# Three score buffers, a shorter inverse factor and a new order in an attention stage of one core

## Chip, core and metric

One of the eight cores of one Trainium2 chip runs the whole program. The metric is the device time of one execution in microseconds. PE is the matmul engine (TensorE), DVE VectorE, ACT ScalarE, POOL GpSimd, and SP the queue that issues the DMAs.

## What is computed

Attention with a cut on its scores, and two feed-forward layers after it. B = 4 batches, 8 heads, 576 tokens, head size 64, so x has 2304 rows and 512 columns.

```
scores = q @ k.T / 8
scores = where(scores >= max(scores) - tau, scores, -1e9)
attn   = exp(scores - max);  attn = attn / (sum(attn) + 1e-9)
x      = attn @ v                      # heads side by side: 2304 x 512
x      = (silu(x @ w_gate) * (x @ w_val)) @ w_out      # 512 -> 1536 -> 512
out    = relu(x @ w_in)**2 @ w_out2                    # 512 -> 2048 -> 512
```

All products are built from a high and a low part of each operand (kh and kl of a key, and so on), since the matmul's operand types hold too few bits for one part.

## The kernel before

The kernel first does the attention, beside it part of the first feed-forward layer, and then the rest of both layers. It is written with a planner: the program below is traced in program order, and the planner puts each engine's instructions into a fixed queue at build time. It goes by priority (the place in the program, moved forward or back by the numbers in the tables `early0` for batch 0 and `early` for the later ones: a positive number brings a step forward, a negative one puts it back by so many places) and by when each step is ready in its own model. On the chip each queue runs in that order and waits for semaphores. `issue_after` puts an instruction behind another one of the same queue, without a wait for its end.

The attention works on 144 tiles of 128 query rows: per batch four pairs of heads, and nine tiles a pair (four of each head, and one, "T", that holds the last 64 rows of both). Turn i of the loop at line 919 takes these steps on the tiles around i, in this order:

- RED (L685, VectorE): the maximum of a tile's scores, less tau.
- CUT (L693, ScalarE): cuts the scores against it, into z. It is the last reader of the score buffer.
- EXP (L701, ScalarE): exponential into e, and the row sum.
- RCP of tile i-1 (L706, VectorE): r = 1/sum, and from batch 1 on a second VectorE instruction, rs = r * 32768 (L709).
- NORM of tile i-1 (L717, GpSimd): e * rs in fp16, the high part of `both`.
- LO of tile i-2 (L764, VectorE): what the fp16 number lacks, the low part of `both`. It reads e and the high part.
- XT of tile i-2 (L768): a DMA transpose of `both` into `pt`, issued by SP.
- QK of tile i+1 (L675, PE): four matmuls (eight for a T tile) into a score buffer.
- `work(i)`: the attention product of a part (AV, L787, 14 matmuls, six turns after its tile), and one group of the first feed-forward layer (L257, 12 matmuls, or L299, 15) when its inputs are there and the credit of 2600 columns a turn allows. These groups are called fill work below.
- The steps that prepare the next pair of heads (`pair_steps`): load raw q and k, scale and split the query (L592, L598), split the key (kh on ScalarE, kl on GpSimd at L77), copy the rest rows (`tail`), and for the values (`value_steps`, `values`) copies on ScalarE, differences on GpSimd and two DMAs into `vb` (L519, L520).

PSUM has eight banks. A score buffer takes two, so the two of them (`sps`) take four. The other four (`bank`) hold, in batch 0, transposed tiles in the first two and AV in the others; from tile 40 on all four go round among AV and the feed-forward groups (class `Mm`). A group's bank is read by ScalarE, VectorE or both after its last matmul: tanh (L277) and an add (L278) for a gate group, a product (L287) for a value group, a copy (L796) and an add (L802) for an AV, a copy (L69) for an output group. These are emitted one turn or more after the group.

Of the kernel before, what the change touches and what calls it, by code (L numbers as in the profile page):

```python
# [10 lines left out]
F32 = mybir.dt.float32  # L11
# [6 lines left out]
AF = mybir.ActivationFunctionType  # L18
# [4 lines left out]
P = 128  # L23
# [60 lines left out]
def attention_moe(tc, qk, values_, tau, w1, w2, out, cfg):  # L84
# [349 lines left out]
    psum = p1.enter_context(tc.tile_pool(name="psum", bufs=1, space=PSUM))  # L434
    bank = [psum.tile([P, 512], F32, name=f"bank{j}") for j in range(4)]
    mp1 = Mm(bank[3:])
# [30 lines left out]
    def raw_head(h):  # L467
        return rawp.tile([P, 2 * S], F32, name=f"raw{h}", tag=f"raw{h % 2}")
# [53 lines left out]
    def first_pair():  # L522

        for h in range(2):
# [56 lines left out]
            yield s2  # L581

    def pair_steps(p):

        raws = [raw_head(2 * p + j) for j in range(2)]

        def query(j):
            hd, q = head(2 * p + j), raws[j][:, :S]
            if p < NPAIR:
                nc.gpsimd.tensor_scalar(hd["qs"], q, scalar1=qscale, scalar2=1.0, op0=ALU.mult, op1=ALU.mult)  # L590
            else:
                nc.scalar.activation(hd["qs"], q, AF.Copy, scale=qscale)  # L592

        def key(j):
            hd, q = heads[2 * p + j], raws[j][:, :S]
            ops.copy(cfg["kh"], hd["kh"], raws[j][:, S:])
            low = hd["qs"][D:, :]
            nc.vector.scalar_tensor_tensor(  # L598
                low, q[D:, :], qscale[D:, :], low.bitcast(F32), op0=ALU.mult, op1=ALU.subtract
            )  # L600

        def key_low(j, c):
            hd = heads[2 * p + j]
            ops.sub(cfg["kl"], hd["kl"][:, c], raws[j][:, S:][:, c], hd["kh"][:, c].bitcast(F32))

        halves_ = (slice(0, HS), slice(HS, S))
        nc.sync.dma_start(raws[0], qk[2 * p])
        yield None
        nc.sync.dma_start(raws[1], qk[2 * p + 1])
        yield None  # L610
        query(0)
        yield None
        key(0)
        yield None
        key_low(0, halves_[0])
        yield None
        key_low(0, halves_[1])
        tail(heads[2 * p])
        yield None
        if p < NPAIR:  # L620
            values(heads[2 * p], 2 * p)
        query(1)
        yield "next"
        key(1)
        key_low(1, halves_[0])
        yield None
        key_low(1, halves_[1])
        tail(heads[2 * p + 1])
        if p < NPAIR:
            values(heads[2 * p + 1], 2 * p + 1)  # L630
        yield None
# [3 lines left out]
    def value_steps(i):  # L635
        p, k = divmod(i, 9)
        if k == 6 and NPAIR <= p + 1 < B * NPAIR:
            rawv[p + 1] = rawp.tile([P, 2 * VW], F32, name=f"rawv{p + 1}", tag="rawv")
            nc.sync.dma_start(rawv[p + 1], values_[p + 1])
        if k in (3, 5) and NPAIR <= p < B * NPAIR:  # L640
            h = 2 * p + (k == 5)
            values(heads[h], h, rawv[p])

# [16 lines left out]
    st = [dict() for _ in range(NTILE + 8)]  # L660

    def QK(t):
        b, p, i = tiles[t]
        kind, c = ORDER[i]
        ha, hb = (heads.get(b * H + 2 * p + j) for j in range(2))
        sp = sps[t % 2]
        st[t]["s"] = sp
# [29 lines left out]
    def EXP(t):  # L697
        e = es[t % len(es)]
        st[t]["e"] = e
        sum_ = sm.tile([P, 1], F32, name=f"sum{t}", tag="sum")  # L700
        ex = nc.scalar.activation(e, st[t]["z"], AF.Exp, scale=-SLOPE, accum_out=sum_)  # L701
        st[t].update(sum=sum_, exp=ex.ins)

    def RCP(t):
        r = st[t]["r"] = sm.tile([P, 1], F32, name=f"r{t}", tag="r")
        nc.vector.reciprocal(r, st[t]["sum"])  # L706
        if way(t) == "VV":
            rs = st[t]["rs"] = sm.tile([P, 1], F32, name=f"rs{t}", tag="rs")
            nc.vector.tensor_scalar(rs, r, scalar1=UNIT, scalar2=None, op0=ALU.mult)  # L709

    def NORM(t):
        e = st[t]["e"][:, :S]
        r = st[t]["r"]
        if way(t) == "VV":
            a = st[t]["both"] = both[(t + 1) % len(both)]
            rs = st[t]["rs"]
            norm = nc.gpsimd.tensor_scalar(a[:, :S], e, scalar1=rs, scalar2=1.0, op0=ALU.mult, op1=ALU.mult)  # L717
            st[t]["norm"] = norm.ins
            return
# [41 lines left out]
    def LO(t):  # L761

        e, a, r = (st[t][x] for x in ("e", "both", "rs"))
        nc.vector.scalar_tensor_tensor(a[:, S:], e[:, :S], r, a[:, :S], op0=ALU.mult, op1=ALU.subtract)  # L764
# [154 lines left out]
    for i in range(NTILE + late):  # L919
# [3 lines left out]
        if i == cfg["three"] + lag:  # L923
            mp1.banks = deque(bank[2:])
        if i == 9 * NPAIR + lag + 2:
            mp1.banks.extend(bank[:2])
        if i >= cfg["ldat"] and (i % cfg["lev"] == 0 or i >= 9 * NPAIR):
# [23 lines left out]
        at_(mp1.flush, "A", name="FA")  # L951
        if i + 1 < NTILE:
            at_(QK, i + 1)
        work(i)
# [676 lines left out]
def pack(inputs):  # L1631
# [14 lines left out]
    def cols(w, nf):  # L1646
# [48 lines left out]
    "early": {  # L1695
        "TR": 8, "LD": -21, "FD": 4, "NEG": -4, "FA": -19, "PL": -12, "PS": -25, "PH": 6, "LS": 64, "RCP": -8,
        "FP": -40, "NORM": -25, "LP": -100,
    },
# [27 lines left out]
```

## Time and profile before

| | us |
|---|---|
| median of 3 runs | 1162.25 |
| lowest and highest | 1160.58, 1162.57 |
| profiled execution | 1160.94 |
| its span, first to last instruction | 1159.1 |

The page of the profile gives busy times for the whole span. The table by stage gives them for stretches of it, here the three batches with fill work (from the cut of tile 36 to that of tile 143), what is left of the attention, and the rest. The views of waits name, for an engine, which line stood idle and which instruction ended that; the view by line gives counts and mean durations; the timeline gives single instructions in order of time.

### The profile page before, as it was taken

To read this page: it belongs to the slowest core of one execution; us is meant where nothing else is said; L and a number is where in the kernel's file an instruction comes from. 1 tells how busy PE (TensorE), PEld (TensorE's weight loads), DVE (VectorE), ACT (ScalarE), POOL (GpSimd) and SP (SyncE) were. 2 spreads that over 40 slices of the span, in tenths; PEclk is the share of its full clock that TensorE was granted. 3 is DMA by queue.
4 is the path that set the end of the run, shared out by engine and by line. 5 is a ranking of instruction groups with operands and counts; after the bars stand their busy time and mean duration, and the time that the engine had idled before them with its cause. 6 is when DMAs were issued, how large, how long until landed. Compare 5 with 4: busy or idle time off the path is not lost.

```text
span 1159.1 us, 18607 instructions
## 1 busy us (share of the span) xinstructions
PE 1085.5 (94%) x6224; PEld 958.6 (83%) x6224; DVE 886.2 (76%) x2103; ACT 640.3 (55%) x1449; POOL 300.1 (26%) x402
## 2 busy tenths in 40 slices
PE   5999888888888889999999999999999999999998
PEld 4787767777777779998888888888999999989997
DVE  5999898888778785589986887679647768866554
ACT  5999776777667663455433443245546555544221
POOL 5866785766656553000000000000000000000000
PEclk9999999899999989999999999999999999999999
DMA  6444887788767653232220134356364544444552
GB/s 192 134 138 138 166 164 166 153 175 171 138 149 145 134 113 56 65 100 83 82 88 13 37 119 161 102 163 247 144 210 164 181 144 169 162 156 143 183 172 82
DMA packets 177024, 159.43 MB, mean 138 GB/s; under 512 B 133792, under 2 KB 138144, under 8 KB 176928
## 3 DMA queue, kind: packets, MB, share of 16 engines
q1 hardware_dynamic: 176784, 158.24, 49.5%
q8 instruction: 49, 0.80, 0.3%
q14 instruction: 47, 0.39, 0.1%
q10 hardware_dynamic: 144, 0.00, 0.0%
HBM read 100.93 MB, written 22.28 MB: 106 GB/s over the span
## 4 chain that ended last, share of the span: by engine, by line
PE 61%; DVE 3%; POOL 1%; issue 1%; ACT 1%; POOLq 0%; ACTq 0%
PE mm L257 18%; PE mm L1536 17%; PE mm L1483 14%; PE mm L299 9%; PE bank L257 1%; PE bank L299 1%; PE bank L787 1%; DVE st__113 L685 0%; POOL both L717 0%; DVE right L77 0%; DVE sum L1369 0%; ACT z L693 0%; DVE both L764 0%; DVE h L1470 0%; DVE wa L77 0%
## 5 line engine op out<-in xcount | busy, mean ns | idle before, releaser
L693 ACT ACTIVATE z<-s,thr 128x576 f32<-128x576 f32 x144 | 106.1, 737 | 77.0 <-DVE st__113 L685 42.5
L764 DVE SCALAR_TENSOR_TENSOR both<-e,rs,both 128x576 f16<-128x576 f32 x108 | 108.1, 1003 | 42.5 <-POOL both L717 41.7
L675 PE MATMUL s<-kh,qs 128*128 128x288 f32 x256 | 86.8, 352 | 44.9 <-ACT z L693 38.2
L257 PE MATMUL mm<-xs,wa 128*128 128x512 f32 (+2 forms) x672 | 125.8, 347 | 0.5 <-ACT x L69 0.5
L685 DVE TENSOR_SCALAR_CACHE_REDUCE st__113<-s,tau_c 128x576 bf16<-128x576 f32 x144 | 116.3, 808 | 10.3 <-ACT vs L69 5.8
L257 PEld LDWEIGHTS mm<-xs,wa 128*128 128x128 f32 x672 | 109.5, 188 | 15.7 <-ACT x L69 0.7
L717 POOL TENSOR_SCALAR both<-e,rs 128x576 f16<-128x576 f32 x108 | 87.5, 812 | 69.0 <-DVE rs L709 26.9
L257 PE MATMUL bank<-xs_m,wa 128*128 128x288 f32 x576 | 93.0, 309 | 8.8 <-DVE xs_m L77 3.7
L701 ACT ACTIVATE e<-z 128x577 f32<-128x577 f32 x144 | 98.4, 683 | 4.1 <-DVE both L764 0.3
L675 PEld LDWEIGHTS s<-kh,qs 128*128 128x128 f32 x256 | 50.6, 198 | 57.2 <-ACT z L693 48.3
L257 PEld LDWEIGHTS bank<-xs_m,wa 128*128 128x128 f32 x576 | 84.2, 198 | 11.9 <-DVE xs_m L77 7.6
L675 PE MATMUL s<-kl,qs 128*128 128x288 f32 x256 | 76.0, 311 | 0.0
L1553 DVE TENSOR_TENSOR xF<-xF,mm 128x512 f32<-128x512 f32 x54 | 36.9, 684 | 51.0 <-PE mm L1536 51.0
L257 PE MATMUL mm<-xs,wb 128*128 128x512 f32 (+1 forms) x360 | 74.9, 368 | 0.0
L257 PEld LDWEIGHTS mm<-xs,wb 128*128 128x128 f32 x360 | 62.8, 188 | 11.3
L69 ACT ACTIVATE wb<-wf 128x256 fp32r<-128x256 f32 x82 | 34.0, 415 | 65.3 <-DVE wf L1138 38.7
L1536 PE MATMUL mm<-wb,wx 128*128 128x512 f32 x270 | 67.3, 389 | 0.0
L1483 PE MATMUL mm<-right,wb 128*128 128x384 f32 x348 | 65.3, 335 | 1.2 <-DVE right L77 1.2
L1135 ACT ACTIVATE wf<-wr 128x256 f32<-128x256 f32 x64 | 27.6, 433 | 66.3 <-DMA wr<-in_w_dram 51.3
L1470 DVE TENSOR_TENSOR h<-mm,h 128x384 f32<-128x384 f32 x72 | 39.6, 551 | 30.4 <-PE mm L1483 30.4
L1483 PEld LDWEIGHTS mm<-right,wb 128*128 128x128 f32 x348 | 60.8, 188 | 1.9 <-DVE right L77 1.4
L77 POOL TENSOR_TENSOR kl<-raw,kh 128x288 fp32r<-128x288 f32 x62 | 60.4, 991 | 5.9 <-ACT kh L69 5.9
(159 smaller groups left out, 2630.3 us busy)
## 6 DMA issues: line engine op xcount, KB each, us to landing
wr<-in_w_dram SPq DMA_DIRECT2D x106, 256.0 KB, 3.0
raw<-in_qk_dram SPq DMA_DIRECT2D x30, 576.0 KB, 4.2
xF<-in_w_dram SPq DMA_DIRECT2D x30, 256.0 KB, 3.2
right<-kept1T SPq DMA_DIRECT2D x8, 768.0 KB, 5.3
right<-kept0T SPq DMA_DIRECT2D x7, 768.0 KB, 5.6
right<-kept SPq DMA_DIRECT2D x6, 768.0 KB, 4.7
right<-kept2T SPq DMA_DIRECT2D x6, 768.0 KB, 5.6
wa<-kept2T SPq DMA_DIRECT2D x6, 768.0 KB, 5.3
```

Source lines behind the costliest of these rows:

```text
L77: e.tensor_tensor(out, a, b, op=ALU.subtract)
L257: mm(pt[:, :n], w[:, a, col + c * P : col + (c + 1) * P], xs[:, b, c, :], start=(i == 0), stop=(i == len(TERMS) - 1),)
L299: mm(pt[:, :n], ws[k][:, a, 2 * DM + m * P : 2 * DM + (m + 1) * P], us[k][:, b, :], start=(k == 0 and i == 0), stop=(k == ahead and i == 2),)
L675: mm(sp[:, cols], l, r[:, cols], start=(n_ == 0), stop=(n_ == len(pairs) - 1),)
L685: red = nc.vector.tensor_scalar(st_, st[t]["s"][:, :S], scalar1=tau_c, scalar2=None, op0=ALU.subtract, op1=ALU.max, accum_out=th)
L693: nc.scalar.activation(z[:, :S], st[t]["s"][:, :S], AF.Prelu, bias=st[t]["thr"], scale=-1.0, alpha=1 / SLOPE)
L701: ex = nc.scalar.activation(e, st[t]["z"], AF.Exp, scale=-SLOPE, accum_out=sum_)
L717: norm = nc.gpsimd.tensor_scalar(a[:, :S], e, scalar1=rs, scalar2=1.0, op0=ALU.mult, op1=ALU.mult)
L764: nc.vector.scalar_tensor_tensor(a[:, S:], e[:, :S], r, a[:, :S], op0=ALU.mult, op1=ALU.subtract)
L1470: return ("D", read(lambda: nc.vector.tensor_tensor(h, bank[:, :BK], h, op=ALU.add), bank))
L1483: mm(bank[:, :BK], w[:, a, c * P : (c + 1) * P], t[:, b, c, :], start=(n == 0 and x in ("11", "12", "S1")), stop=(n == 5), skip_group_chec ...
L1536: mm(pt, u[:, b, s * P : (s + 1) * P], w[a], start=(half == 0 and j == 0 and i == 0), stop=(half == 1 and j == 1 and i == 2),)
```

## The change

From batch 1 on (tile `THIRD` = 38) the scores go round in three buffers, the third made of the first two of the four other banks, and QK runs two tiles ahead of the loop; AV and the feed-forward groups keep the other two banks, as they had at the end of batch 0. ScalarE divides the row sum by 32768 right behind the exponential, so the reciprocal is the scaled factor and L709 goes; NORM and LO read it. The loads of q and k are issued right behind the last reader of their buffer, a load of values behind that of the next queries, and the value copies behind the exponential of the tile before. The second head's key step comes one step earlier. In the table of priorities RCP and NORM lose their entries (-8, -25) and LO gets -10.

```diff
-    bank = [psum.tile([P, 512], F32, name=f"bank{j}") for j in range(4)]
+    two = psum.tile([P, 1024], F32, name="bank01")
+    bank = [two[:, :512], two[:, 512:], *(psum.tile([P, 512], F32, name=f"bank{j}") for j in range(2, 4))]
...
+    raws, loads = {}, {}
     def pair_steps(p):
-        raws = [raw_head(2 * p + j) for j in range(2)]
+        def load(h):
+            if h not in raws and h < B * H:
+                raws[h] = raw_head(h)
+                loads[h] = nc.sync.dma_start(raws[h], qk[h]).ins
...
-        nc.sync.dma_start(raws[0], qk[2 * p])
-        yield None
-        nc.sync.dma_start(raws[1], qk[2 * p + 1])
+        load(2 * p)
+        load(2 * p + 1)
...
         tail(heads[2 * p])
+        load(2 * p + 2)
         yield None
         if p < NPAIR:
             values(heads[2 * p], 2 * p)
         query(1)
+        yield None
+        key(1)
         yield "next"
-        key(1)
         key_low(1, halves_[0])
+        key_low(1, halves_[1])
         yield None
-        key_low(1, halves_[1])
         tail(heads[2 * p + 1])
+        load(2 * p + 3)
...
-            nc.sync.dma_start(rawv[p + 1], values_[p + 1])
+            with tc.issue_after(loads[2 * p + 2]):
+                nc.sync.dma_start(rawv[p + 1], values_[p + 1])
...
-            values(heads[h], h, rawv[p])
+            with tc.issue_after(st[i - 1]["exp"]):
+                values(heads[h], h, rawv[p])
...
+    THIRD = 9 * NPAIR + 2
+    sps3 = [*sps, two[:, 512 - HS :]]
     def QK(t):
-        sp = sps[t % 2]
+        sp = sps[t % 2] if t < THIRD else sps3[(t - THIRD) % 3]
...
         ex = nc.scalar.activation(e, st[t]["z"], AF.Exp, scale=-SLOPE, accum_out=sum_)
+        if way(t) == "VV":
+            part = sm.tile([P, 1], F32, name=f"part{t}", tag="part")
+            nc.scalar.activation(part, sum_, AF.Copy, scale=1 / UNIT)
+            sum_ = part
...
         nc.vector.reciprocal(r, st[t]["sum"])
-        if way(t) == "VV":
-            rs = st[t]["rs"] = sm.tile([P, 1], F32, name=f"rs{t}", tag="rs")
-            nc.vector.tensor_scalar(rs, r, scalar1=UNIT, scalar2=None, op0=ALU.mult)
...
-        if i == 9 * NPAIR + lag + 2:
-            mp1.banks.extend(bank[:2])
...
-        if i + 1 < NTILE:
-            at_(QK, i + 1)
+        for j in (i + 1, i + 2) if i == THIRD + 1 else (i + 2,) if i > THIRD else (i + 1,):
+            if j < NTILE:
+                at_(QK, j)
...
-        "TR": 8, "LD": -21, "FD": 4, "NEG": -4, "FA": -19, "PL": -12, "PS": -25, "PH": 6, "LS": 64, "RCP": -8,
-        "FP": -40, "NORM": -25, "LP": -100,
+        "TR": 8, "LD": -21, "FD": 4, "NEG": -4, "FA": -19, "PL": -12, "PS": -25, "PH": 6, "LS": 64,
+        "FP": -40, "LO": -10, "LP": -100,
```

## Rows read from the trace of the kernel before

**Rows 1.** The page, busy us, share of the span and instructions of each engine.

```profile
PE 1085.5 (94%) x6224; PEld 958.6 (83%) x6224; DVE 886.2 (76%) x2103; ACT 640.3 (55%) x1449; POOL 300.1 (26%) x402
```

**Rows 2.** Table by stage: stretch, length, busy us by engine, granted clock, DMA.

```profile
101.20:215.30 114.10, 97.26 (x677) 85.57 (x676) 98.09 (x243) 83.17 (x190) 80.72 (x100) 0.99 0.80 164
215.30:326.10 110.80, 94.19 (x660) 82.48 (x660) 95.09 (x231) 81.29 (x182) 73.08 (x90) 0.95 0.78 157
326.10:438.10 112.00, 95.22 (x661) 83.69 (x662) 91.22 (x228) 77.19 (x176) 65.89 (x87) 0.95 0.66 134
438.10:472.40 34.30, 34.30 (x263) 32.92 (x261) 12.38 (x28) 9.84 (x27) 8.17 (x12) 1.00 0.23 38
472.40:1159.00 686.60, 680.88 (x3495) 604.02 (x3493) 505.87 (x1164) 305.60 (x681) 0.00 (x0) 1.00 0.39 134
```

**Rows 3.** Waits of PE, 101.2 to 438.1: total us, times, longest us.

```profile
PE s L675 <- ACT z L693: 36.8, 30, 3.7
```

**Rows 4.** Waits of ScalarE, the same stretch.

```profile
ACT z L693 <- DVE st__113 L685: 42.5, 33, 4.2
ACT z L693 <- DVE r L706: 17.2, 7, 3.7
ACT z L693 <- DVE rs L709: 13.3, 11, 3.0
```

**Rows 5.** Waits of VectorE, the same stretch.

```profile
DVE both L764 <- POOL both L717: 39.4, 52, 2.2
...
DVE st__113 L685 <- PE s L675: 1.0, 2, 0.8
```

**Rows 6.** Waits of GpSimd, the same stretch.

```profile
POOL both L717 <- DVE rs L709: 24.6, 21, 2.3
POOL both L717 <- ACT e L701: 13.1, 8, 2.4
```

**Rows 7.** VectorE by line, the same stretch: count, busy us, mean ns, idle before.

```profile
L764 DVE SCALAR_TENSOR_TENSOR both<-e,rs,both 128x576 f16<-128x576 f32 x105 | 105.2, 1004 | 40.1 <-POOL both L717 39.4
...
L709 DVE TENSOR_SCALAR rs<-r 128x1 f32<-128x1 f32 x106 | 15.7, 149 | 1.4
```

**Rows 8.** The tile `both`, the same stretch: ns least/median/most.

```profile
L764 DVE SCALAR_TENSOR_TENSOR both<-e,rs,both x105: 803/819/1489, 105.6 to 435.9; 128x576 f16<-128x576 f32 x105
```

**Rows 9.** Timeline, all engines: start, us, engine, line, what; idle before and releaser.

```profile
394.31 0.40 PE L675 MATMUL s<-kh,qs 128*128 128x288 f32 x1 [0.43 <-ACT z L693]
...
394.94 1.76 PE L257 MATMUL bank<-xs_m,wa 128*128 128x288 f32 x12
...
395.87 2.16 POOL L77 TENSOR_TENSOR kl<-raw,kh 128x288 fp32r<-128x288 f32 x2 [0.34 <-ACT kh L69]
...
398.02 0.74 POOL L717 TENSOR_SCALAR both<-e,rs 128x576 f16<-128x576 f32 x1
...
398.79 0.82 DVE L764 SCALAR_TENSOR_TENSOR both<-e,rs,both 128x576 f16<-128x576 f32 x1 [1.06 <-POOL both L717]
...
399.89 0.82 DVE L685 TENSOR_SCALAR_CACHE_REDUCE st__113<-s,tau_c 128x576 bf16<-128x576 f32 x1
...
400.81 0.74 ACT L693 ACTIVATE z<-s,thr 128x576 f32<-128x576 f32 x1 [2.75 <-DVE st__113 L685]
401.19 0.46 DVE L287 SCALAR_TENSOR_TENSOR m_th<-m_th,bank 128x288 f32<-128x288 f32 x1
...
401.60 0.40 PE L675 MATMUL s<-kh,qs 128*128 128x288 f32 x1 [2.47 <-ACT z L693]
...
402.92 1.35 DVE L764 SCALAR_TENSOR_TENSOR both<-e,rs,both 128x576 f16<-128x576 f32 x1 [0.31 <-POOL both L717]
...
403.62 1.31 POOL L77 TENSOR_TENSOR rawv<-rawv,vs 128x320 f32<-128x320 f32 x1
```

**Rows 10.** ScalarE by line and shape, 101.2 to 438.1: its smallest instructions.

```profile
L701 ACT ACTIVATION_READ_ACCUMULATOR e<-z 128x1 f32 x107 | 20.4, 191 | 0.0
...
L796 ACT ACTIVATE xF<-bank 64x64 f32<-64x64 f32 x11 | 2.4, 219 | 0.3
```

**Rows 11.** Waits in the SP queue, 160 to 450: total us, times, longest us.

```profile
SPq L607 <- POOL kl L77: 11.7, 6, 3.0
```

More of the change, by code (lines that the diff above doesn't have):

```diff
@@ L581, in first_pair @@
             yield s2
+    raws, loads = {}, {}
     def pair_steps(p):
-        raws = [raw_head(2 * p + j) for j in range(2)]
+        def load(h):
+            if h not in raws and h < B * H:
+                raws[h] = raw_head(h)
+                loads[h] = nc.sync.dma_start(raws[h], qk[h]).ins
         def query(j):
-            hd, q = head(2 * p + j), raws[j][:, :S]
+            hd, q = head(2 * p + j), raws[2 * p + j][:, :S]
             if p < NPAIR:
@@ L594, in key @@
         def key(j):
-            hd, q = heads[2 * p + j], raws[j][:, :S]
-            ops.copy(cfg["kh"], hd["kh"], raws[j][:, S:])
+            hd, q = heads[2 * p + j], raws[2 * p + j][:, :S]
+            ops.copy(cfg["kh"], hd["kh"], raws[2 * p + j][:, S:])
             low = hd["qs"][D:, :]
@@ L603, in key_low @@
             hd = heads[2 * p + j]
-            ops.sub(cfg["kl"], hd["kl"][:, c], raws[j][:, S:][:, c], hd["kh"][:, c].bitcast(F32))
+            ops.sub(cfg["kl"], hd["kl"][:, c], raws[2 * p + j][:, S:][:, c], hd["kh"][:, c].bitcast(F32))
         halves_ = (slice(0, HS), slice(HS, S))
-        nc.sync.dma_start(raws[0], qk[2 * p])
-        yield None
-        nc.sync.dma_start(raws[1], qk[2 * p + 1])
+        load(2 * p)
+        load(2 * p + 1)
         yield None
@@ L715, in NORM @@
             a = st[t]["both"] = both[(t + 1) % len(both)]
-            rs = st[t]["rs"]
-            norm = nc.gpsimd.tensor_scalar(a[:, :S], e, scalar1=rs, scalar2=1.0, op0=ALU.mult, op1=ALU.mult)
+            norm = nc.gpsimd.tensor_scalar(a[:, :S], e, scalar1=r, scalar2=1.0, op0=ALU.mult, op1=ALU.mult)
             st[t]["norm"] = norm.ins
@@ L761, in LO @@
     def LO(t):
-        e, a, r = (st[t][x] for x in ("e", "both", "rs"))
+        e, a, r = (st[t][x] for x in ("e", "both", "r"))
         nc.vector.scalar_tensor_tensor(a[:, S:], e[:, :S], r, a[:, :S], op0=ALU.mult, op1=ALU.subtract)
```

## The prediction, made before the change was run

> **What bounds the kernel now.** I read the page first: PE is busy for 94% of the span [rows 1], so what can be won is PE's idle time, and the question is where it lies. The table by stage answers that [rows 2]: from 438.1 us to the end PE idles 5.7 us in 721, while in the three attention stretches of batches 1 to 3 (101.2 to 438.1 us, 336.9 us, 108 tiles, 3.12 us a tile) it is busy 97.26 + 94.19 + 95.22 = 286.7 us and idle 50.2. The change acts almost only there. In the same stretch DVE is busy 284.4 us, ACT 241.7, POOL 219.7: PE and DVE stand level at 85%.
>
> The waits, engine by engine, tell who sets the pace. PE's one large wait is the score matmul (QK, L675) for the cut on ScalarE (CUT, L693) to give its score buffer free: 36.8 us [rows 3]. ScalarE waits at the cut for VectorE: 42.5 + 17.2 + 13.3 us [rows 4]. VectorE waits for GpSimd's normalised tile (NORM, L717) before it can form the low part (LO, L764): 39.4 us in 52 of 105 tiles, and for the scores of PE hardly at all, 1.0 us [rows 5]. GpSimd in turn waits for VectorE's scaled factor (L709) 24.6 us and for the exponential 13.1 us [rows 6]. So VectorE's queue sets the pace: its own 284.4 us plus 39.4 us behind GpSimd are 96% of the stretch. The timeline shows one case [rows 9]: the scores of tile 131 are begun at 394.31, but VectorE stands 1.06 us at LO until NORM ends at 398.76 (GpSimd had the key's low part before it), only then runs the maximum of tile 131 (399.89), ScalarE had waited 2.75 us for that, and PE 2.47 us for ScalarE.
>
> **The change, part by part.** All terms are for that stretch; the sign is that of the time.
>
> *A. The scaled factor leaves VectorE.* 106 instructions at 149 ns, 15.7 us [rows 7], go from the queue that sets the pace. I take -15.7; bounds 0 (were PE to become the limit at once) and -15.7.
>
> *B. Order: RCP and NORM are no longer put back by 8 and 25 places, LO is put back by 10.* NORM comes earlier on GpSimd, before key and value work that was ahead of it (the 2.16 us of kl ahead of it in [rows 9]), and VectorE reaches LO later. What can go is the 39.4 us of [rows 5]. A queue's order is fixed at build time, and 13.1 us of NORM's own waits are for the exponential [rows 6], which doesn't move. I take half, -20; bounds 0 and -39.4.
>
> *C. LO beside GpSimd.* LO takes 0.82 us in [rows 9] at 398.79 and 1.35 us at 402.92, where GpSimd works on m_u and rawv; the median is 0.819 and the mean 1.004 us [rows 7, 8], so slow ones already cost 105 x 0.185 = 19.4 us. A LO that waits has GpSimd just finishing beside it; one that comes later finds it in its next instruction. Bounds: all at 0.82, -19.4; all at 1.35, 105 x 0.346 = +36. I take half as much again as today, +9, nearer to the mean of today than to either end. The Trainium skill (SBUF — State Buffer, "Who interferes with whom") says that a VectorE instruction with two SBUF inputs contends with a GpSimd instruction that reads SBUF; LO is of that form, and the two durations agree with it. By that rule term C would be at its upper end for every LO that overlaps, which is rival 2.
>
> *D. ScalarE forms sum/32768.* 108 more instructions of one column. The nearest rows are the accumulator read, 191 ns, and the 64x64 copy, 219 ns [rows 10]: 20 to 24 us more on ScalarE. Behind it in the queue stand the next cut and the copies; ScalarE's 73 us of waiting for VectorE [rows 4] cover it, and if that cover is gone it costs up to +24. On the path to NORM one ScalarE instruction replaces one of VectorE: 0.2 against 0.15 us. I take +2.
>
> *E. Three score buffers, two banks for the rest.* QK of tile i+2 is issued in turn i, in three buffers. It waits for the cut of tile i-1, just as QK of tile i+1 in two buffers did: PE's 36.8 us [rows 3] don't go by the count, only by a faster VectorE. What the third buffer gives is a tile's more slack between QK and the maximum, and that wait is 1.0 us [rows 5]. The price: the attention products, the gate/value groups and the output groups turn in two banks, where before it was four. I paired each such group of PE (113 from 101.2 us on) with its last reader in the timeline: mean 2.26 us from first to last matmul, and 4.37 us more until the bank is read; in [rows 9] the group at 394.94 ends at 396.70 and is read until 401.65. With two banks 69 of the 113 groups would have begun before their bank was free, by 134 us in all. Most of that delay is queue order which PE's lead permits, and PE has 36.8 us of waits to spend on it. Bounds: 0, all absorbed; +40, rival 1. A gain by E alone I bound with -1.0. I take +10, a quarter.
>
> *F. Loads and values.* The loads of q and k are issued as soon as the buffer is read, behind GpSimd's kl. The SP queue holds them in order, so a waiting load holds up the DMA transposes and vb copies behind it: such waits are 11.7 us now [rows 11], and PE would only feel them through the products six turns later. The value copies are put behind the previous tile's exponential on ScalarE, which keeps the cut from standing behind them; they wait for GpSimd anyway. Key work of the second head comes one step earlier, same instructions. I take 0; bounds -8 and +5 (a transposed tile that lands late).
>
> *G. The tail.* From 438.1 to 472.4 PE is busy without a gap [rows 2]; with two banks a group's readers have the other group's time, 1.76 us [rows 9], for a tanh and an add of about 0.45 each. I take +1; bounds 0 and +8 (some 20 groups by 0.4).
>
> Sum: -15.7 - 20 + 9 + 2 + 10 + 0 + 1 = -13.7 us. The profiled execution took 1160.9 us (its span 1159.1, 1.8 around it): 1147.2. The median of the runs is 1.3 us above the profiled one, so I say **1148.5 us**, -1.2%. PE would then be idle about 36 of 323 us in the stretch, which it can be.
>
> **Rivals.**
> 1. *The bank rotation takes the place of the freed waits; slower.* A bank is held 2.26 + 4.37 = 6.6 us; two banks give a group each 3.3 us, 113 x 3.3 = 375 against 336.9 us: +38 to +40. With A to D at -25 this ends near +13 to +15, 1175 us. For it: today's mean. Against it: the readers are late because nothing pressed them, and ScalarE and VectorE reach them in the next two turns. It decides if a group's readers stay later than about 3.7 us behind its end: 2 x 2.98 us (336.9/113) less 2.26.
> 2. *GpSimd beside VectorE takes back what the order gives.* LO always at 1.35: -15.7 - 39.4 + 36 + 13 (D, E, G) = -6: 1156 us.
> 3. *VectorE is freed fully and PE becomes the bound.* A and B at their ends with C, D and G as in the sum: -15.7 - 39.4 + 9 + 2 + 1 = -43; PE's idle time is 50.2 us and a twentieth of the stretch stays idle, so about -33: 1129 us.
> 4. *The order isn't moved in the queues* (NORM still behind kl and m_u, which are ready sooner). Then A alone stands against D, E and G: -15.7 + 13 = -3, 1159.5, not to be told from no change.
>
> **How the numbers follow.** Forecast (1138 to 1154) 0.40, rival 3 0.12, rival 2 0.12, rival 4 0.11, rival 1 0.25. About 0.2%, 2.3 us, is what a measurement of this kernel can tell from no change, so of rival 4 a third falls to faster: faster 0.68, same 0.08, slower 0.24 (rival 1, less the part of it in which the banks only eat the gain). The range reaches half into rival 3 and to the price of rival 1: 1130 to 1176, which leaves out some 0.06 and 0.1. It takes in the bounds of each term alone; all of them at one end together it doesn't.
>
> **What would show it.** Right: from about 105 us to the last cut some 323 instead of 337 us; no scaled-factor instruction on VectorE and one more of about 0.2 us on ScalarE per tile (A, D); VectorE's wait at LO at or under 20 us (B); LO's mean at 1.05 to 1.15 us (C); PE's waits at QK under 30 us, and waits of the groups L257, L299 and L787 for ScalarE's and VectorE's reads of a bank of 5 to 20 us, where now there are hardly any (E); none of these after the last cut (G). Wrong: PE waiting over 40 us for banks, or ScalarE and VectorE standing at tanh and adds for PE (rival 1); LO's mean near 1.35 (rival 2); a wait at LO still near 39 us (rival 4); PE idle under 25 us in the stretch (rival 3). The forecast also falls if the transposed tiles come late, seen as PE waiting for DMA.

## The result: 0.9% slower, and where the 10 us lie

The changed kernel took 1171.9 us in the median (1170.7 to 1174.2), the one before 1162.4 beside it on the same chip: ratio 1.0086, 95% interval 1.0067 to 1.0106. The profiled execution has a span of 1168.9 us against 1159.1.

The table by stage puts the loss in place. It is cut as in [rows 2], at the cut of tile 36 and at that of tile 143, and at the first matmul of the second stage (columns: stretch, length, busy us of PE, PEld, DVE, ACT, POOL, granted clock, DMA share, GB/s). After:

```profile
99.10:442.50 343.40, 283.83 (x1987) 249.77 (x1986) 277.37 (x589) 253.67 (x655) 221.67 (x279) 0.97 0.75 150
442.50:483.20 40.70, 39.23 (x281) 36.17 (x280) 11.60 (x27) 11.07 (x29) 8.36 (x12) 0.96 0.13 25
```

Before, cut in the same way:

```profile
101.20:438.10 336.90, 286.67 (x1998) 251.75 (x1998) 284.40 (x700) 241.65 (x548) 219.70 (x277) 0.96 0.75 152
438.10:473.20 35.10, 34.65 (x264) 33.04 (x261) 12.38 (x28) 10.63 (x28) 8.17 (x12) 1.00 0.23 38
```

Batch 0 ends 2.1 us sooner, batches 1 to 3 take 6.5 us more, the tail up to the second stage 5.6 us more, and the rest is the same within 0.2 us: +9.8. Of the 6.5 us some 2 are work moved over a border from batch 0 (the run on the loads, below). VectorE has 111 instructions less in the attention stretch and 7.0 us less to do, and still the stretch is longer. PE stands idle 59.6 us in it, where it was 50.2.

The waits say what became of PE's 36.8 us at the scores [rows 3]. Waits of PE after, 99.1 to 442.5 (total us, times, longest us):

```profile
PE bank L800 <- DVE xF L815: 19.3, 13, 4.0
PE bank L257 <- DVE xF L815: 10.2, 9, 2.4
PE bank L257 <- DVE m_th L278: 9.4, 11, 1.8
PE bank L299 <- DVE xF L815: 9.0, 3, 4.1
...
PE bank L800 <- DVE m_th L278: 2.7, 3, 1.1
...
PE s L688 <- ACT z L706: 0.5, 2, 0.3
```

The wait for the cut is gone (0.5 us, and 1.0 us for the third buffer). In its place PE waits some 51 us for VectorE to read the two banks in which attention products (L800) and feed-forward groups (L257, L299) go round. The waits of the other three engines, the same stretch, each line from its own view:

```profile
DVE both L777 <- POOL both L730: 51.5, 61, 2.4
```
```profile
ACT z L706 <- DVE st__112 L698: 60.2, 42, 3.8
```
```profile
POOL both L730 <- DVE r L723: 60.3, 44, 4.4
```

VectorE waits longer at the low part (LO) than before, 51.5 against 39.4 us [rows 5], though the new order was to shorten that. GpSimd waits 60.3 us for the factor, where it was 24.6 [rows 6]. ScalarE's waits at the cut are the exception: with another 2.2 us for the reciprocal they come to 62.4 us, where they were 73.0 [rows 4].

One place of the timeline after shows all of it at once (start, us, engine, what; idle before and releaser):

```profile
321.77 0.74 POOL L730 TENSOR_SCALAR both<-e,r 128x576 f16<-128x576 f32 x1 [3.03 <-DMA pt<-both]
...
322.55 1.33 DVE L777 SCALAR_TENSOR_TENSOR both<-e,r,both 128x576 f16<-128x576 f32 x1 [2.38 <-POOL both L730]
...
323.91 0.42 DVE L815 SCALAR_TENSOR_TENSOR xF<-bank,xF 64x256 f32<-64x256 f32 x1
324.36 0.16 DVE L723 RECIPROCAL r<-part 128x1 f32<-128x1 f32 x1
324.39 1.85 PE L299 MATMUL bank<-m_u,wa 128*128 128x288 f32 x12 [2.46 <-DVE xF L815]
324.44 0.80 DVE L698 TENSOR_SCALAR_CACHE_REDUCE st__112<-s,tau_c 128x576 bf16<-128x576 f32 x1
...
325.29 0.74 ACT L706 ACTIVATE z<-s,thr 128x576 f32<-128x576 f32 x1 [0.95 <-DVE st__112 L698]
```

The high part (NORM) of tile 105 waits on GpSimd 3.03 us for a buffer that a DMA transpose still reads. The low part of that tile stands at the head of VectorE's queue and waits 2.38 us for NORM. Behind it in the queue stand the add that frees a bank (L815), for which PE waits 2.46 us, and the maximum of tile 107, for which ScalarE waits; the scores of tile 107 were begun at 321.24. A wait at LO is paid by whatever is queued behind it. That NORM waits for a transpose is the rarer reason in this kernel, three places in all, against 44 waits for the reciprocal:

```profile
POOL both L730 <- DMA pt<-both: 5.9, 3, 3.0
```

### The profile page after: what moved, and what is told of

Read it like the earlier page. It is cut to its first block, busy times and chain, and to the rows that moved or that the text cites. A ratio compares the mean times of both kernels' runs of the same rounds, so it can differ in the third digit from the quotient of the medians.

```text
span 1168.9 us, 18539 instructions
## 1 busy us (share of the span) xinstructions
PE 1088.5 (93%) x6224; PEld 959.6 (82%) x6224; DVE 879.7 (75%) x1995; ACT 653.0 (56%) x1557; POOL 302.7 (26%) x402
## 4 chain that ended last, share of the span: by engine, by line
PE 56%; DVE 11%; POOL 9%; issue 6%; ACT 5%; DMA 3%; POOLq 0%; ACTq 0%; DVEq 0%; SPq 0%
PE mm L257 17%; PE mm L1548 15%; PE mm L1495 11%; PE mm L299 7%; POOL both L730 4%; DVE both L777 2%; PE bank L257 2%; POOL kl L77 2%; DMA pt<-both 2%; PE bank L299 2%; DVE st__112 L698 2%; PE bank L800 2%; DMA wr<-in_w_dram 1%; ACT z L706 1%; ACT e L714 1%
## 5 line engine op out<-in xcount | busy, mean ns | idle before, releaser
L777 DVE SCALAR_TENSOR_TENSOR both<-e,r,both 128x576 f16<-128x576 f32 x108 | 110.1, 1022 | 53.9 <-POOL both L730 53.4
L257 PE MATMUL mm<-xs,wa 128*128 128x512 f32 (+2 forms) x672 | 125.7, 347 | 0.5 <-ACT x L69 0.5
L257 PEld LDWEIGHTS mm<-xs,wa 128*128 128x128 f32 x672 | 109.4, 188 | 15.7 <-ACT x L69 0.7
L257 PE MATMUL bank<-xs_m,wa 128*128 128x288 f32 x576 | 94.2, 310 | 24.0 <-DVE m_th L278 9.7
L730 POOL TENSOR_SCALAR both<-e,r 128x576 f16<-128x576 f32 x108 | 92.7, 859 | 70.2 <-DVE r L723 62.8
L257 PEld LDWEIGHTS bank<-xs_m,wa 128*128 128x128 f32 x576 | 82.2, 195 | 33.7 <-DVE m_th L278 11.7
L706 ACT ACTIVATE z<-s,thr 128x576 f32<-128x576 f32 x109 | 80.2, 736 | 46.0 <-DVE st__112 L698 43.8
L698 DVE TENSOR_SCALAR_CACHE_REDUCE st__112<-s,tau_c 128x576 bf16<-128x576 f32 x109 | 88.1, 808 | 5.2 <-PE s L688 3.3
L688 PE MATMUL s<-kh,qs 128*128 128x288 f32 x210 | 68.0, 337 | 9.4 <-DVE qs L545 6.3
L257 PE MATMUL mm<-xs,wb 128*128 128x512 f32 (+1 forms) x360 | 74.9, 368 | 0.0
L257 PEld LDWEIGHTS mm<-xs,wb 128*128 128x128 f32 x360 | 62.9, 188 | 11.3
L688 PE MATMUL s<-kl,qs 128*128 128x288 f32 x210 | 61.8, 309 | 0.0
L1479 ACT ACTIVATE h<-mm 128x384 f32<-128x384 f32 x72 | 34.9, 484 | 47.8 <-PE mm L1495 47.4
L800 PE MATMUL bank<-pt,vs 128*128 128x256 f16 (+1 forms) x240 | 39.9, 297 | 22.9 <-DVE xF L815 19.3
```

Of the source, the lines that this page charges most:

```text
L257: mm(pt[:, :n], w[:, a, col + c * P : col + (c + 1) * P], xs[:, b, c, :], start=(i == 0), stop=(i == len(TERMS) - 1),)
L688: mm(sp[:, cols], l, r[:, cols], start=(n_ == 0), stop=(n_ == len(pairs) - 1),)
L698: red = nc.vector.tensor_scalar(st_, st[t]["s"][:, :S], scalar1=tau_c, scalar2=None, op0=ALU.subtract, op1=ALU.max, accum_out=th)
L706: nc.scalar.activation(z[:, :S], st[t]["s"][:, :S], AF.Prelu, bias=st[t]["thr"], scale=-1.0, alpha=1 / SLOPE)
L730: norm = nc.gpsimd.tensor_scalar(a[:, :S], e, scalar1=r, scalar2=1.0, op0=ALU.mult, op1=ALU.mult)
L800: mm(o[:, :n], v, pt[:, k if k < 9 else k - 9, lo : lo + n], start=(k == 0), stop=(k == 13))
```

## Experiments

Each kernel is held against runs of the kernel before on the same chip, whose median lay between 1160.6 and 1162.0 us there. Two variants that were not run side by side are compared through that, so a difference between them is good to 2 or 3 us, by their intervals. The theories: 1, the rotation of groups in two banks costs the time; 2, the new priorities do; 3, ScalarE's added instruction does; 4, any new queue order does; 5, formed after the first runs, the place of LO in VectorE's queue does.

### Two banks alone

```diff
-        if i == 9 * NPAIR + lag + 2:
-            mp1.banks.extend(bank[:2])
```

> The kernel before with one line less: attention products and feed-forward groups keep two banks in batches 1 to 3; two score buffers, the two freed banks stay unused. Theory 1 (the bank rotation makes the change slower): 8 to 20 us slower than before, about 1170 to 1182, PE waiting 30 to 60 us for reads of a bank at L257, L299, L787 and under 15 us at the scores, where it was 36.8. Theory 2 (the order of reciprocal, high part and low part makes it slower): within 4 us of before, since PE's waits only change their name.

1169.5 us, ratio 1.0076 (1.0061 to 1.0091): +8.8 us. Waits of PE, 100.7 to 447.7:

```profile
PE bank L787 <- DVE xF L802: 14.7, 10, 3.0
PE s L675 <- ACT z L693: 9.1, 11, 2.8
PE bank L299 <- DVE xF L802: 8.0, 4, 2.6
PE bank L257 <- DVE m_th L278: 7.6, 7, 3.1
PE bank L257 <- DVE xF L802: 6.2, 6, 3.8
```

Theory 1 holds for this step: 36.5 us of these waits are for banks, and they are not simply PE's old wait under a new name, since the kernel is slower.

### Three score buffers, two banks, scores one tile ahead

```diff
...
+    THIRD = 9 * NPAIR + 2
+    sps3 = [*sps, two[:, 512 - HS :]]
...
-        sp = sps[t % 2]
+        sp = sps[t % 2] if t < THIRD else sps3[(t - THIRD) % 3]
...
-        if i == 9 * NPAIR + lag + 2:
-            mp1.banks.extend(bank[:2])
```

> The kernel before with three score buffers and two banks, scores still one tile ahead. PE's score matmul then waits for a cut two tiles back in place of one. Theory 1 (rotation): like two banks alone, 5 to 12 us slower, PE waiting 30 to 50 us for banks and under 5 us at the scores. If the third buffer pays for the banks: within 3 us of before.

1171.6 us, 1.0087 (1.0072 to 1.0102): as slow as two banks alone, within the intervals. PE's wait at the scores falls to 2.9 us, the waits for banks are 18.5 + 10.1 + 6.4 + 5.3 us, and nothing is won: the third buffer takes away a wait that the banks give back. Three score buffers beside four other banks can't be run, since they would need ten of the eight banks; what a third buffer is worth by itself stays unknown.

### The factor alone

```diff
+        if way(t) == "VV":
+            part = sm.tile([P, 1], F32, name=f"part{t}", tag="part")
+            nc.scalar.activation(part, sum_, AF.Copy, scale=1 / UNIT)
+            sum_ = part
...
-            nc.vector.tensor_scalar(rs, r, scalar1=UNIT, scalar2=None, op0=ALU.mult)
...
```

NORM and LO then read r.

> The kernel before with the inverse factor alone: ScalarE divides the sum, VectorE's second instruction goes, all else as before. Term A of the prediction: 10 to 15 us faster, 1147 to 1152. Theory 1 and theory 2: faster by some 3 to 12 us. Theory 3 (the added ScalarE instruction sits on the path from exponential to high part): same or slower, with GpSimd's wait for the factor above 40 us where it was 24.6.

1166.9 us, 1.0060 (1.0043 to 1.0077): +6.3 us from an edit that takes 106 instructions off VectorE. Its waits, 100.9 to 442.7, VectorE, PE, then two of GpSimd:

```profile
DVE both L764 <- POOL both L717: 57.4, 58, 2.8
```
```profile
PE s L675 <- ACT z L693: 40.5, 36, 3.8
```
```profile
POOL both L717 <- DVE r L710: 48.6, 39, 2.2
...
POOL both L717 <- DMA pt<-both: 13.9, 8, 2.1
```

VectorE is busy 274.2 us against 284.4, and waits 18.0 us longer at LO: the time saved and 8 us more go into a wait. PE's idle time in the stretch is no longer than before, 50.0 against 50.2 us, and its busy time 5.2 us longer for the same 1998 matmuls, so this loss is read from VectorE's waits and not from PE's.

### The priorities alone

```diff
-        "TR": 8, "LD": -21, "FD": 4, "NEG": -4, "FA": -19, "PL": -12, "PS": -25, "PH": 6, "LS": 64, "RCP": -8,
-        "FP": -40, "NORM": -25, "LP": -100,
+        "TR": 8, "LD": -21, "FD": 4, "NEG": -4, "FA": -19, "PL": -12, "PS": -25, "PH": 6, "LS": 64,
+        "FP": -40, "LO": -10, "LP": -100,
```

> The kernel before with the new priorities alone: reciprocal and high part not put back, low part put back by 10. Term B: 10 to 25 us faster, VectorE's wait at the low part at or under 20 us. Theory 2: 5 to 12 us slower, that wait at 45 us or more. Theory 1: same or faster.

1161.1 us, 1.0003 (0.9993 to 1.0012), VectorE's wait at LO 42.0 us. Neither term B nor theory 2: with the numbers moved by 8, 25 and 10 places, another line stands at 350 of the 2103 places of VectorE's queue, and the time is the same.

### Everything but the score buffers

From the changed kernel:

```diff
-    two = psum.tile([P, 1024], F32, name="bank01")
-    bank = [two[:, :512], two[:, 512:], *(psum.tile([P, 512], F32, name=f"bank{j}") for j in range(2, 4))]
+    bank = [psum.tile([P, 512], F32, name=f"bank{j}") for j in range(4)]
...
-        sp = sps[t % 2] if t < THIRD else sps3[(t - THIRD) % 3]
+        sp = sps[t % 2]
...
+        if i == 9 * NPAIR + lag + 2:
+            mp1.banks.extend(bank[:2])
...
-        for j in (i + 1, i + 2) if i == THIRD + 1 else (i + 2,) if i > THIRD else (i + 1,):
-            if j < NTILE:
-                at_(QK, j)
+        if i + 1 < NTILE:
+            at_(QK, i + 1)
```

> The changed kernel with its score buffers undone: two score buffers, scores one tile ahead, four banks; factor, loads and priorities as changed. Theory 1: 10 to 20 us faster than the changed kernel, that is 1150 to 1160, below before. Theory 2: still slower than before, 1166 to 1172, VectorE waiting about 50 us at the low part.

1168.4 us, 1.0067 (1.0052 to 1.0082), so with four banks the rest of the change is still 7.8 us slower than before. VectorE's and PE's largest waits, 98.8 to 448.0:

```profile
DVE both L773 <- POOL both L726: 65.8, 65, 3.5
```
```profile
PE s L684 <- ACT z L702: 49.9, 37, 4.0
```

Theory 1 alone falls here. The score buffers and banks thus add only 2 to 4 us in the changed kernel: the loss at the banks (8.8) and this one don't add up to 16 us there. PE waits 49.9 us for score buffers here and some 51 us for banks in the changed kernel, so it seems to spend the same time at either; no run shows that by itself.

### A spare instruction on ScalarE, and another order without other work

```diff
+        if way(t) == "VV":
+            part = sm.tile([P, 1], F32, name=f"part{t}", tag="part")
+            nc.scalar.activation(part, sum_, AF.Copy, scale=1 / UNIT)
```

> The kernel before plus ScalarE's instruction sum/32768 in each of the 108 tiles of batches 1 to 3, its result unread; VectorE keeps both of its instructions. Theory 3 (the instruction on ScalarE costs): 6 to 12 us slower, as with the factor alone (+6.3) or a little more. Theory 4 (the planner's new queue order costs, whatever is edited): slower by about as much as the spare control c4_reorder, 0 to 8 us. Cover as argued in the prediction: within 2 us of before.

1161.2 us, 0.9999 (0.9990 to 1.0008). 107 instructions of 196 ns on ScalarE cost nothing that can be measured, so the cover named in term D was there. As nothing reads the result, the other half of theory 3, that the instruction lengthens the path to NORM, isn't tested here; it falls with the kernel that has the instruction on that path and is 19.8 us faster (LO behind the maximum, below).

```diff
-    "ldat": 8,
+    "ldat": 9,
```

> The kernel before with one number changed that removes and adds no instruction: the first weight load of batch 0 starts one turn later (turn 9). The planner then places some 1,000 of PE's and 470 of VectorE's rows otherwise. Theory 4 (order alone is worth several us): off by 4 us or more in either direction, mostly in the attention stage of batches 1 to 3. Theories 1 and 3: within 2 us of before.

1161.1 us, 0.9999 (0.9989 to 1.0008). In this kernel 67 places of VectorE's queue hold another line, in the one with the new priorities 350, and neither time moves. Theory 4, that any new order costs, falls; what a chosen order is worth, the runs below show.

### The high part from the plain reciprocal

```diff
-        if way(t) == "VV":
-            rs = st[t]["rs"] = sm.tile([P, 1], F32, name=f"rs{t}", tag="rs")
-            nc.vector.tensor_scalar(rs, r, scalar1=UNIT, scalar2=None, op0=ALU.mult)
...
-            rs = st[t]["rs"]
-            norm = nc.gpsimd.tensor_scalar(a[:, :S], e, scalar1=rs, scalar2=1.0, op0=ALU.mult, op1=ALU.mult)
+            norm = nc.gpsimd.tensor_scalar(a[:, :S], e, scalar1=r, scalar2=UNIT, op0=ALU.mult, op1=ALU.mult)
             st[t]["norm"] = norm.ins
+            rs = st[t]["rs"] = sm.tile([P, 1], F32, name=f"rs{t}", tag="rs")
+            nc.vector.tensor_scalar(rs, r, scalar1=UNIT, scalar2=None, op0=ALU.mult)
```

The scaled factor, for LO alone, comes after the high part.

> The kernel before with the high part formed from the plain reciprocal (GpSimd multiplies by 32768 as its second scalar), and VectorE's scaled factor after it, needed by the low part alone. No instruction more or less; GpSimd no longer waits for the second VectorE instruction, which was 1.0 us after the first. If the chain factor, high part, low part is what VectorE waits for: 5 to 15 us faster, VectorE's wait at the low part under 30 us. If the planner puts the low part right behind the high part anyhow: within 4 us of before, that wait at 35 to 50 us.

1158.7 us, 0.9976 (0.9966 to 0.9987): 2.8 us faster, VectorE's wait at LO 31.8 us. The time is that of the second reading (within 4 us of before), the wait lies between the two. The edit takes the second VectorE instruction off the path to NORM without an instruction on ScalarE. GpSimd now waits 17.1 us for DMA transposes, where it was 2.4.

### The low part behind the maximum

The timelines show where LO of tile t starts against the maximum of tile t+2, in 106 tiles of each kernel. LO came first in 20 tiles before (its waits there 15.0 us), in 39 with the factor alone (43.8 us), in 43 after the change (33.9 us), in 48 without the score buffers (50.6 us). It is the factor that does it, and not the priorities: with the priorities alone LO came first in 25 tiles (26.0 us), with the whole change but the factor in 18, with the spare instruction on ScalarE in 22. My reading, which no run shows by itself: without the removed instruction NORM is ready sooner in the planner's model, and LO is placed sooner too, ahead of the maximum that ScalarE and PE wait for. The test puts LO behind that maximum, an order only:

```diff
-            at_(LO, i - 2)
+            with tc.issue_after(st[min(i, NTILE - 1)]["red"]):
+                at_(LO, i - 2)
```

On the factor alone (the expectation's "some 12" tiles before the change are 20 by the trace):

> The factor on ScalarE alone (measured 6.3 us slower than before), and the low part of tile t is queued on VectorE behind the maximum of tile t+2, an order without a wait. In the queue of the factor variant the low part stands ahead of that maximum in some 40 of 108 tiles, before the change in some 12. Theory 5 (a low part that waits for GpSimd, queued ahead of the maximum which the cut and PE wait for, is what the factor variant loses): back to before or below, 1150 to 1162, VectorE's wait at the low part under 25 us where it was 57.4. Theory 3 (ScalarE's instruction in the path to the high part): still 4 to 8 us slower than before.

1142.2 us, 0.9834 (0.9818 to 0.9850): 19.8 us faster than before, some 25 less than the same without that line, and below the 1150 to 1162 that theory 5 foretold. Waits of VectorE, ScalarE and PE, 101.0 to 419.3:

```profile
DVE both L764 <- POOL both L717: 16.5, 26, 2.2
```
```profile
ACT z L693 <- DVE st__113 L685: 34.8, 42, 2.9
```
```profile
PE s L675 <- ACT z L693: 24.0, 26, 2.7
```

LO's wait falls from 57.4 to 16.5 us, and with it the two waits behind it, ScalarE's for the maximum from 65.5 us and PE's for the cut from 40.5. On the whole change:

> The whole change, with the low part of tile t behind the maximum of tile t+2. Theory 1 and theory 5 together: the part of the two banks stays, 6 to 12 us slower than before less what the order gives: 1160 to 1170, PE waiting 30 to 50 us for banks, VectorE under 25 us at the low part, where it was 51.5. Theory 5 alone: 1150 to 1160.

1148.7 us, 0.9888 (0.9873 to 0.9902): the same line takes 23 us from the changed kernel, to below both expectations. PE still waits for banks, but less than the 30 to 50 us expected (99.1 to 422.2; the largest of them):

```profile
PE bank L257 <- DVE m_th L278: 8.7, 6, 2.5
PE bank L800 <- DVE xF L815: 7.2, 6, 3.1
PE bank L299 <- DVE xF L815: 4.7, 2, 2.4
```

On the variant with the plain reciprocal:

> The high part from the plain reciprocal (measured 2.8 us faster than before), with the low part of tile t behind the maximum of tile t+2 too. Theory 5: faster than that by 3 to 12 us more, 1146 to 1156, VectorE's wait at the low part under 20 us. If PE or GpSimd sets the pace by then: within 3 us of 1158.6.

1145.8 us, 0.9862 (0.9847 to 0.9877), LO's wait 15.3 us, as theory 5 has it. On the kernel before, by itself:

> The kernel before with one line: the low part of tile t queued behind the maximum of tile t+2; VectorE keeps its scaled factor. If the order itself is what was missing: 8 to 16 us faster than before, 1146 to 1154, and the factor on ScalarE is worth the rest up to 1142. If the order only repairs what the factor variant broke: within 3 us of before.

1151.2 us, 0.9914 (0.9899 to 0.9929). So the order alone brings 10.1 us, and with the order right the factor on ScalarE brings some 9 more (0.9834 against 0.9914), the sign that term A had. Without it the same factor costs 6.3 us: what it is worth hangs on where LO stands.

### The loads alone

The loads of heads and values as the change has them, in the kernel before (the core of it):

```diff
-        nc.sync.dma_start(raws[0], qk[2 * p])
-        yield None
-        nc.sync.dma_start(raws[1], qk[2 * p + 1])
+        load(2 * p)
+        load(2 * p + 1)
...
+        load(2 * p + 2)
...
+            with tc.issue_after(loads[2 * p + 2]):
+                nc.sync.dma_start(rawv[p + 1], values_[p + 1])
...
+            with tc.issue_after(st[i - 1]["exp"]):
+                values(heads[h], h, rawv[p])
```

> The kernel before with the loads, the second head's key step and the value copies as changed, nothing else. Term F of the prediction: within 3 us of before. If the value copies behind the exponential hold up GpSimd or the transposes: 3 to 8 us slower, with ScalarE waiting over 10 us at the value copies, 8.3 before.

1162.4 us, 1.0009 (1.0000 to 1.0019): term F was right to about 1 us. Its batch 0 ends 3.2 us sooner and its batches 1 to 3 take 5.4 us more, with the whole span 0.6 us longer; the early end of batch 0 in the change, which every kernel with these loads has, is work moved over a border.

### The banks once more, with the order mended

> All of the change but the score buffers (four banks, scores one tile ahead), with the low part behind the maximum. If the two banks cost as much with the order mended as without: 6 to 10 us faster than the same with three buffers (1148.7), that is 1138 to 1143. If third buffer and banks balance once VectorE is quicker: 1146 to 1151.

All of the change but the score buffers, with LO behind the maximum: 1140.5 us, 0.9820 (0.9804 to 0.9836), against 1148.7 with three buffers and two banks. The banks cost 8 us here too. The edit is the one line of order above, in that kernel.

The factor back on VectorE, all else as in the change:

```diff
-        if way(t) == "VV":
-            part = sm.tile([P, 1], F32, name=f"part{t}", tag="part")
-            nc.scalar.activation(part, sum_, AF.Copy, scale=1 / UNIT)
-            sum_ = part
...
+        if way(t) == "VV":
+            rs = st[t]["rs"] = sm.tile([P, 1], F32, name=f"rs{t}", tag="rs")
+            nc.vector.tensor_scalar(rs, r, scalar1=UNIT, scalar2=None, op0=ALU.mult)
...
```

> The changed kernel with the factor on VectorE again: three buffers, two banks, loads and priorities as changed. If banks and factor add up: 4 to 8 us faster than the changed kernel, 1163 to 1167. If they are the same loss seen twice: within 3 us of the changed kernel.

The change with the factor back on VectorE: 1168.0 us, 1.0050 (1.0036 to 1.0065), against 1.0086 for the change. The factor's own share in it is about 4 us, less than the 6.3 it costs alone: the two losses add up in part, between the two expectations.

### Priorities on top, and a fourth buffer for high and low part

In the factor variant with LO behind the maximum:

```diff
-        "TR": 8, "LD": -21, "FD": 4, "NEG": -4, "FA": -19, "PL": -12, "PS": -25, "PH": 6, "LS": 64, "RCP": -8,
-        "FP": -40, "NORM": -25, "LP": -100,
+        "TR": 8, "LD": -21, "FD": 4, "NEG": -4, "FA": -19, "PL": -12, "PS": -25, "PH": 6, "LS": 64, 
+        "FP": -40, "LP": -100,
```

> The factor on ScalarE, the low part behind the maximum, and reciprocal and high part no longer put back (no entries in the table). If the high part now comes earlier in time: 1136 to 1141, below 1142.2. If GpSimd's order isn't on the path any more: within 3 us of 1142.2.

Factor, order and the priorities of RCP and NORM: 1139.5 us, 0.9813 (0.9796 to 0.9829), 2.7 us below the same with the old priorities; the intervals overlap, and both readings allow it, so it decides nothing. In it GpSimd waits 17.2 us for DMA transposes before NORM (2.4 before the change): `both` has three buffers, each held until its transpose has landed. That wait is also in the factor variant (13.9 us), and theory 5 had not asked about it. Two kernels give `both` a fourth buffer, one on the factor variant, one on the factor variant with order and priorities. To find the room, the maximum's unused output now goes to a place that nothing else uses in this stage:

```diff
-    both = [ptp.tile([P, 2 * S], F16, name=f"both{j}", tag=f"both{j}") for j in range(3)]
+    both = [ptp.tile([P, 2 * S], F16, name=f"both{j}", tag=f"both{j}") for j in range(4)]
...
-    st_ = ptp.tile([P, S], mybir.dt.bfloat16, name="st_")
+    st_ = x2[0][1][:, 3, LAST - HS :].bitcast(BF16)
```

> The factor on ScalarE alone, with four buffers for high and low parts in place of three; room for it comes from writing the maximum's unread element output into a part of x2 that isn't used yet. If GpSimd's wait for the transposes is what the factor variant loses: back to within 2 us of before, 1159 to 1163. If the low part's place in the queue is (theory 5): still 4 to 7 us slower than before, with GpSimd's wait for the transposes gone.

1157.7 us, 0.9971 (0.9961 to 0.9981), 9 us below the factor variant with three buffers, and GpSimd's waits for transposes are gone. The order of lines and operations in the queues of all engines is the same as there, so apart from where the maximum's unused output lies only the buffers differ. The expectation from theory 5, still 4 to 7 us slower, fell; the other one (1159 to 1163) was passed by a little. LO still waits:

```profile
DVE both L764 <- POOL both L717: 49.0, 58, 2.3
```
```profile
POOL both L717 <- DVE r L710: 50.2, 41, 2.2
```

LO still comes ahead of the maximum in 39 tiles, with 37.1 us of waits there, more than the kernel before has, and the time is below before. So LO's place alone doesn't set the time, and the factor's loss has two keys, either of which opens it: NORM not held up by a transpose (-9 us), or nothing urgent queued behind the LO that waits for NORM (-25 us).

> The fastest kernel so far (factor on ScalarE, low part behind the maximum, reciprocal and high part not put back, 1139.5) with four buffers for high and low parts. GpSimd waits 17.2 us for transposes in it. If that is on the path: 2 to 8 us faster, 1131 to 1137. If VectorE's and PE's own work set the pace: within 2 us of 1139.5.

1131.7 us, 0.9746 (0.9732 to 0.9761): 29 us faster than before, the fastest version here, and 8 us below the same with three buffers; GpSimd's waits for transposes are 2.3 us. Its row by stage, where PE is idle 28.4 us and VectorE 35.8 us:

```profile
100.90:408.20 307.30, 278.91 (x1997) 246.20 (x1997) 271.54 (x595) 254.72 (x655) 242.28 (x279) 0.99 0.87 167
```

## Why the prediction was wrong

It said 1148.5 us and faster; the time is 1171.9, slower. That this lies inside the range, near the price of rival 1, is luck: rival 1 added +38 for the banks to -25 for the terms A to D, where the banks measured +8.8 and the factor +6.3, the two overlapping.

*Terms A and B failed, and they carried the sign.* Term A took VectorE's 96% (busy or behind GpSimd) for a queue that gets shorter by what is removed. Alone the factor is +6.3 us, not -15.7: a queue that waits for another engine gets shorter only up to the next wait, and LO's wait grew by 18.0 us. Term B took a place in the table of priorities for a place in the queue. Alone the priorities are worth 0, not -20: LO "put back by 10" came ahead of the maximum in 25 tiles, where it had been 20, and VectorE's wait at it is 42.0 us, not half of 39.4. In the whole change it came ahead in 43 tiles, and there the removed factor did it, since with the factor back on VectorE it is 18. The wrong step was the same in both: I read from [rows 5, 9] that VectorE waits at LO and asked how to shorten the wait, not what stands behind LO and in which order. The rows had it: in [rows 9] the maximum, the cut and PE all stand behind one LO. With that order mended A is some -9 us, and the order itself -10.

*Term E was right in size.* Two banks alone cost +8.8 against +10. The waits for banks were 51 us, though, beyond the 5 to 20 that I had named and past rival 1's sign of over 40, so the place was rival 1's. And PE's waits for a score buffer, which I had held not to go by the count, fell from 36.8 to 1.5 us in the change and to 9.1 with two banks alone; what held is that nothing is gained by it, as PE then waits for banks.

*Term C* was +2 us, not +9: LO's mean is 1.026 us after [rows 7: 1.004]. The line of VectorE after:

```profile
L777 DVE SCALAR_TENSOR_TENSOR both<-e,r,both 128x576 f16<-128x576 f32 x106 | 108.5, 1026 | 52.1 <-POOL both L730 51.5
```

Rival 2 thus had no part in it. A slow LO isn't one that overlaps with GpSimd, but one that starts while an instruction of GpSimd is running: after the change 46 of 50 such took over 0.95 us (mean 1.26), and none of the 15 beside which GpSimd's instruction began later (mean 0.81; 0.82 for the 43 without one); before, it was 42 of 57 and 1 of 12. So overlap alone doesn't make an LO slow. A row of before that overlaps and isn't:

```profile
395.81 0.81 DVE L764 SCALAR_TENSOR_TENSOR both<-e,rs,both 128x576 f16<-128x576 f32 x1
395.87 2.16 POOL L77 TENSOR_TENSOR kl<-raw,kh 128x288 fp32r<-128x288 f32 x2 [0.34 <-ACT kh L69]
```

*Term D*, +2, measured 0 for ScalarE's time (the spare instruction), with the duration foretold (ScalarE after):

```profile
L717 ACT ACTIVATE part<-sum 128x1 f32<-128x1 f32 x107 | 20.8, 194 | 1.0
```

*Term F* held, 1 us. What it left out was the transposes' hold on the buffers of `both`: I asked whether a late transpose holds up a product six turns on, not whether it holds up NORM three tiles on (5.9 us in the change, 13.9 with the factor alone). *Term G* was too small: the tail is 5.6 us longer, not 1. PE idles 1.0 us more in it, 17 more matmuls come behind the last cut, and the granted clock there is 0.96, not 1.00. The banks, by which I had reckoned the term, have little part in it: with two banks alone what follows the last cut is 0.6 us longer than before. The idle time of PE in the stretch, 59.6 us, shows rival 3 (PE the bound) far off. Rival 4's condition, that the order isn't moved, was near the truth for the priorities; its price was not, as it kept A at -15.7.

What stays open: why the order alone takes 10 us from the kernel before while the plain reciprocal takes 3 (in that kernel LO came ahead of the maximum in 32 tiles, with 24.6 us of waits, and GpSimd waited 17.1 us for transposes, which may be what ate the rest); how the fourth buffer wins 9 us while LO still waits 49.0 us; and which of the changed parts together send more matmuls behind the last cut.

## What to carry to other kernels

Before taking work or waits off the engine that sets the pace, list what is queued behind its longest wait; an instruction that may wait should stand behind the ones that others wait for, and one line that orders them was worth more here (10 us alone, 25 with the factor) than the removed instructions (9 us at best). Under a planner a removed instruction is also a new order, and a moved priority may not give the one that was meant: compare the queues, not the tables. A buffer's hold time, transposes and all, bounds how far a producer can be moved forward. Banks taken from one rotation are paid for by waits on its readers, 8 to 9 us here, alone and with the order mended.

## What the runs showed of the chip that I had not expected

A DMA transpose of `both` (128x1152, two bytes each) occupies the SP queue for 1.3 us in the median and lands 3.2 us after its issue at the least, 3.4 in the median and 6.3 at the most, in the kernel before; three buffers at 3.1 us a tile leave little room for that, and GpSimd waited for it 2.4 us before, 13.9 with the factor alone and 31.7 with the order mended and all of the change but the score buffers. A ScalarE instruction of one column took 194 to 196 ns, and 107 of them were free. PE's granted clock was highest where PE idled least, 0.99 over the stretch of the fastest kernel with 28.4 us idle, but it doesn't follow idle time: the three stretches before have 16.6 to 16.8 us of it each at 0.99, 0.95 and 0.95 [rows 2], and the changed kernel idles more than the one before (59.6 against 50.2 us) at 0.97 against 0.96.
